# Attention and swish kernel: kv products as two column tiles, and the chunk of tails moved to the end

## The chip, the cores and the metric

The kernel runs on one core of a Trainium2 chip. The metric is the device time of one execution in microseconds. Durations inside the kernel come from a profile of one execution by the hardware profiler; times called "start" count from the start of the profiled span.

## The reference

The kernel computes a linear attention over 8 batches, 8 heads, 576 positions and a head size of 64, and passes its rows through a two-layer block with a swish. Cut to what matters:

```python
def _attn_ref(q, k, v):                       # (8, 8, 576, 64) each
    q_s = np.exp(q - q.max(-1)); q_s /= q_s.sum(-1)
    k_s = np.exp(k - k.max(2));  k_s /= k_s.sum(2)
    kv = np.einsum('bhsd,bhse->bhde', k_s, v)
    return np.einsum('bhsd,bhde->bhse', q_s, kv)

def _moe_ref(x, w_in, w_out, beta):           # x: (4608, 512)
    h = x @ w_in                              # (4608, 2048)
    g = h * (1.0 / (1.0 + np.exp(-beta * h)))
    return g @ w_out                          # (4608, 512)
```

(the keepdims of the reductions are left out here). The result is 4608 rows of 512 values in float32.

## The kernel before

**Chunks.** The 4608 rows are worked off in nine chunks of 512 rows. Chunks 0 to 7 are the first 512 positions of batches 0 to 7 (`MAIN`). The remaining 64 positions of each batch (`TAIL`) are gathered into one more chunk, number `B` = 8, "the tails". The list `order` (lines 47 to 49) says in which order the chunks run; with `LASTMAIN` it is 0 to 6, then 8, then 7. `LASTC` is the chunk that runs last.

**One chunk.** A chunk has 16 steps, one for each block of 128 of the 2048 hidden values. A step is four products of 512 columns with `w_in_b` (`mm_a`, line 334) into `h`, a tanh on ScalarE (line 344), a multiplication on VectorE (line 346) that gives `g`, and, two steps later (`LAG`), four products of 512 columns with `w_out_b` (`mm_b`, line 362) into the four accumulators of the chunk. After the 16th step `store` evacuates the four accumulators, two on ScalarE (`copy`, line 143) and two on VectorE (line 145), and writes them out.

**Attention.** While chunk n of the order runs, `side(n, u)` puts the attention of the next one between the steps u: the exponentials and sums of q (steps 2 to 5), the exponentials of k and the cast of v (4 and 5), the transposition of q by DMA (`q_xbar`, line 240, step 6), the kv products of batch n + 1 (`kv_mm` and `kv_norm`, steps 8 and 10), and the products of q with kv, which give the input of the next chunk (`x_mm`, steps 11 to 14). In the first stage with `side` (n = 1) the steps up to 10 lie two later. k and v go by the batch n + 1, q by `order[n + 1]`. At step 9 `load_next(n + 2)` issues the loads of the chunk after next on SyncE's queue: either one load of q (line 85) or the eight small ones of the q tails (line 93), and then k and v with their tails (lines 109 and 113).

**kv.** A call of `kv_mm` handles two pairs of heads. For batches 2 to 7 each pair is the sum of five products: four over the 512 main positions (line 286) and one over the tails (line 293). The stationary operand is a 128 by 128 block of exponentials of k, 64 columns for each head of the pair. The moving operand is v of both heads with a column of constants for each, 130 columns. Of the result only the two blocks in which head meets head are used: head 0 in partitions 0 to 63 and columns 0 to 64, head 1 in partitions 64 to 127 and columns 65 to 129. `kv_norm` takes the reciprocal of the sums of k (line 304) and writes the two scaled blocks to `kvp` (line 309), a block-diagonal 128 by 128 matrix for each pair. Batches 0 and 1 use another layout (line 264): a full 128 by 128 stationary operand with zeros and 65 moving columns.

**x.** For a main chunk `x_mm` is one product of 512 columns for each pair (line 314); for the tails it is eight of 64 columns, one for each batch (line 318).

**Stores.** `store` has four branches. Tails that are not last: one tile, four stores of 256 KB on SyncE's queue (line 384). Tails that are last: three tiles, two stores for each, one for each half of the partitions (line 401). A main chunk that is last: four tiles and four stores of 256 KB (line 410), the second on ScalarE's queue. Any other main chunk: two stores of 512 KB (line 418). The order of all instructions on each engine is that of the program; the switches `FIX`, `LASTMAIN` and `COLT` on line 45 choose between variants of it.

Of the kernel before, what the change touches and what calls it, by code (L numbers as in the profile page):

```python
# [17 lines left out]
def kernel(  # L18
# [23 lines left out]
    NW = 2  # L42
    D1 = D + 1
    LAG = 2
    FIX, LASTMAIN, COLT = False, True, False
    NCH = B + 1
    order = list(range(NCH))
    if LASTMAIN:
# [620 lines left out]
```

## Time and profile before

| quantity | value |
|---|---|
| median of 3 runs | 291.6 us (291.25 to 292.26) |
| the profiled execution | 292.26 us |
| its span, first to last instruction | 290.5 us |
| mean granted TensorE clock | 0.997 |
| DMA traffic | 50.06 MB, mean 172 GB/s |
| kv products of batches 2 to 7, lines 286 and 293 | 96 + 24, modelled 0.22 us each |
| 128-column weight load for them, LDWEIGHTS | 98 ns each |

In the profile PE is the matrix engine's stream of products and PEld its weight loads, which run beside the products. DVE is VectorE, ACT ScalarE, POOL GpSimd. SPq and ACTq are the queues from which SyncE and ScalarE issue DMAs. Products are pipelined: the duration shown for one contains its way through the array, so a product can start long before the one ahead of it is shown to end. The distance between the starts of two products says what one of them costs in a full stream.

### The profile page before, as it was taken

The numbers are of one execution on the slowest core, as the hardware profiler recorded it, in microseconds if no ns is written. First come the engines' busy times: TensorE is split into PE (matmuls) and PEld (weight loads), VectorE is DVE, ScalarE is ACT, GpSimd is POOL, SyncE is SP. The second block draws the span as 40 slices with busy tenths as digits, with TensorE's granted clock in tenths as the row PEclk, the third lists the DMA queues.
The fourth block names the chain that finished last, engine by engine and source line by source line (L and its number), as shares of the span: only waits on it lengthen the run. The fifth ranks groups of instructions, "written<-read, shape, count | busy, mean of one in ns | idle before, by whom it ended". The sixth has DMA issues, their size and how long they took to land.

```text
span 290.5 us, 3880 instructions
## 1 busy us (share of the span) xinstructions
PE 278.6 (96%) x1447; PEld 131.0 (45%) x1475; DVE 185.2 (64%) x299; ACT 163.9 (56%) x238; POOL 41.5 (14%) x55
## 2 busy tenths in 40 slices
PE   8779979999999999999999999999999999999994
PEld 2434435445444544454445444544455444444441
DVE  7837596695678546955695469546955595454442
ACT  4853676694387347734682568355944564454341
POOL 4349670300030011001200030003000000000000
PEclk9999999999999999999999999999999999999998
DMA  7999999808941972198119902785381033005003
GB/s 248 376 384 378 377 384 316 252 0 218 315 156 38 309 197 105 47 320 217 72 78 271 272 28 118 172 226 146 144 166 53 1 147 72 0 0 147 0 0 144
DMA packets 56226, 50.06 MB, mean 172 GB/s; under 512 B 26240, under 2 KB 47760, under 8 KB 56208
## 3 DMA queue, kind: packets, MB, share of 16 engines
q1 hardware_dynamic: 56064, 49.56, 55.7%
q8 instruction: 11, 0.18, 0.3%
q10 hardware_dynamic: 144, 0.26, 0.2%
q14 instruction: 7, 0.06, 0.1%
HBM read 36.71 MB, written 9.44 MB: 159 GB/s over the span
## 4 chain that ended last, share of the span: by engine, by line
PE 87%; DMA 4%; DVE 3%; ACT 1%; issue 1%; another core or an unknown queue 1%; SPq 0%; POOL 0%; ACTq 0%
DMA k_st_86<-in_k_dram 2%; DMA w_in_97<-in_moe_w_in_dram 2%; PE acc_2_2486 L362 1%; PE acc_0_2173 L362 1%; PE acc_3_724 L362 1%; PE acc_2_2731 L362 1%; PE acc_0_2484 L362 1%; PE acc_2_2175 L362 1%; PE acc_2_1879 L362 1%; PE acc_0_1877 L362 1%; PE acc_1_1589 L362 1%; PE acc_3_2176 L362 1%; PE acc_0_1588 L362 1%; PE acc_2_1012 L362 1%; PE acc_0_1010 L362 1%; PE acc_0_721 L362 1%
## 5 line engine op out<-in xcount | busy, mean ns | idle before, releaser
L334 PEld LDWEIGHTS <-w_in_b 128*128 128x128 bf16 x576 | 55.3, 98 | 66.7 <-issue 2.7
L158 ACT ACTIVATE ek_144<-k_st_86 64x576 bf16<-64x576 f32 x8 | 5.5, 681 | 1.5 <-DVE eq_189 L231 1.4
L426 PEld LDWEIGHTS <-kvp 128*128 128x128 bf16 x34 | 3.6, 112 | 5.7 <-issue 2.8
L145 POOL CAST va_2209<-v_st_2014 128x2048 bf16<-128x2048 f32 x1 | 1.9, 1918 | 29.1 <-DMA v_st_2014<-in_v_dram 29.1
L145 POOL CAST va_1913<-v_st_1718 128x2048 bf16<-128x2048 f32 x1 | 1.9, 1920 | 28.5 <-DMA v_st_1718<-in_v_dram 28.5
L145 POOL CAST va_1624<-v_st_1429 128x2048 bf16<-128x2048 f32 x1 | 1.9, 1917 | 26.7 <-DMA v_st_1429<-in_v_dram 26.7
L158 ACT ACTIVATE ek_149<-k_st_118 64x576 bf16<-64x576 f32 x8 | 5.4, 675 | 0.0
L145 POOL CAST va_1046<-v_st_836 128x2048 bf16<-128x2048 f32 x1 | 1.9, 1919 | 24.2 <-DMA v_st_836<-in_v_dram 24.2
L145 POOL CAST va_1335<-v_st_1140 128x2048 bf16<-128x2048 f32 x1 | 1.9, 1922 | 22.3 <-DMA v_st_1140<-in_v_dram 22.3
L314 PEld LDWEIGHTS <-kvp 128*128 128x128 bf16 x32 | 3.1, 98 | 4.2 <-DVE kvp L309 1.0
L214 ACT ACTIVATE eq_189<-q_st_83 128x1024 bf16<-128x1024 f32 x2 | 2.1, 1056 | 3.0 <-DMA q_st_83<-in_q_dram 3.0
L145 POOL CAST va_147<-v_st_91 128x576 bf16<-128x576 f32 x4 | 2.7, 668 | 7.8 <-DMA v_st_91<-in_v_dram 7.6
L145 POOL CAST va_783<-v_st_132 128x2048 bf16<-128x2048 f32 x1 | 1.9, 1916 | 12.3 <-DMA v_st_132<-in_v_dram 12.3
L145 POOL CAST w_in_b<-w_in_114 128x1024 bf16<-128x1024 f32 x2 | 3.0, 1536 | 2.1 <-DMA w_in_114<-in_moe_w_in_dram 2.1
L231 DVE TENSOR_TENSOR eq_485<-eq_485,rq_487 128x1024 bf16<-128x1024 bf16 x2 | 3.1, 1542 | 0.0
L334 PE MATMUL h_0_316<-xT_80,w_in_b 128*128 128x512 bf16 x4 | 1.5, 380 | 1.5 <-POOL w_in_b L145 1.3
L145 POOL CAST w_out_b<-w_out_116 128x1024 bf16<-128x1024 f32 x2 | 2.6, 1298 | 1.7 <-DMA w_out_116<-in_moe_w_out_dram 1.7
L145 DVE CAST w_in_b<-w_in_102 128x1024 bf16<-128x1024 f32 x2 | 2.6, 1312 | 0.0
L225 DVE TENSOR_REDUCE rq_748<-eq_746 128x16 f32<-128x1024 bf16 x2 | 2.4, 1214 | 0.3 <-ACT eq_746 L214 0.3
L225 DVE TENSOR_REDUCE rq_487<-eq_485 128x16 f32<-128x1024 bf16 x2 | 2.4, 1213 | 0.3 <-ACT eq_485 L214 0.3
L225 DVE TENSOR_REDUCE rq_191<-eq_189 128x16 f32<-128x1024 bf16 x2 | 2.4, 1215 | 0.2 <-ACT eq_189 L214 0.2
L145 POOL CAST w_out_b<-w_out_100 128x1024 bf16<-128x1024 f32 x2 | 2.1, 1040 | 3.3 <-DMA w_out_100<-in_moe_w_out_dram 3.3
(1460 smaller groups left out, 839.6 us busy)
## 6 DMA issues: line engine op xcount, KB each, us to landing
k_st_86<-in_k_dram SPq DMA_DIRECT2D x4, 288.0 KB, 7.0
v_st_91<-in_v_dram SPq DMA_DIRECT2D x4, 288.0 KB, 7.8
k_st_118<-in_k_dram SPq DMA_DIRECT2D x4, 288.0 KB, 9.7
v_st_124<-in_v_dram SPq DMA_DIRECT2D x2, 576.0 KB, 9.3
q_st_83<-in_q_dram SPq DMA_DIRECT2D x2, 512.0 KB, 4.3
w_in_97<-in_moe_w_in_dram SPq DMA_DIRECT2D x2, 512.0 KB, 6.4
w_out_100<-in_moe_w_out_dram SPq DMA_DIRECT2D x2, 512.0 KB, 8.6
w_in_102<-in_moe_w_in_dram SPq DMA_DIRECT2D x1, 1024.0 KB, 9.3
```

The lines of the kernel that those rows point to most:

```text
L145: eng.tensor_copy(dst, src)
L158: nc.scalar.activation(ek[b][r, j : j + m, :, e * D : (e + 1) * D], k_st[b][r, j : j + m, :].rearrange("p j (i d) -> p j i d", i=RW), ACTF ...
L214: nc.scalar.activation(eq[b][:, :, s * m : (s + 1) * m, :].rearrange("p i h d -> p h i d"), q_st[b][:, s * m : (s + 1) * m, :].rearrange(" ...
L225: nc.vector.tensor_reduce(rq[b][:, 0, :, h], eq[b][:, :, h, :], axis=AX.X, op=ALU.add)
L231: nc.vector.tensor_tensor(eq[b][:, :, h, :], eq[b][:, :, h, :], rq[b][:, 1, :, h].unsqueeze(3).to_broadcast((P, R, m, D)), ALU.mult,)
L314: nc.tensor.matmul(t[:], kvp[:, c, j, :], qsT[c][:, :, j, :])
L334: nc.tensor.matmul(h[:], w_in_b[:, kt, ds(j * P, P)], x_of(c)[:, kt, :], start=(kt == 0), stop=(kt == KT - 1),)
L362: nc.tensor.matmul(acc[st][:], g[:, ds(st * P, P)], w_out_b[:, j, :], start=(j == 0), stop=(j == NJ - 1),)
L426: nc.tensor.matmul(t[:, 0:cols], kvp[:, B - 1, 0, :], kvp[:, B - 1, :, :].rearrange("p j r -> p (j r)")[:, 0:cols],)
```

## The change

Two switches on line 45 are turned; no other line is changed.

```diff
-    FIX, LASTMAIN, COLT = False, True, False
+    FIX, LASTMAIN, COLT = False, False, True
```

With `COLT` the branch at lines 272 to 284 takes the place of lines 285 to 299 for batches 2 to 7:

```python
                for i in range(R + 1):
                    for e in range(2):
                        hd = 2 * j + e
                        nc.tensor.matmul(
                            t[e * D : (e + 1) * D, jl, 0:D1],
                            ek[b][:, i, hd, :] if i < R else ekt[...][:, ds(hd * D, D)],
                            va[b][:, i, hd, :] if i < R else vt[...][:, b % 2, hd, :],
                            start=(i == 0),
                            stop=(i == R),
                            tile_position=(0, e * D),
                        )
```

Each head gets products of its own: a stationary operand of 128 rows by 64 columns, placed in the left or right half of the array by `tile_position`, and 65 moving columns. The heads of a pair alternate. Both results lie in columns 0 to 64, in their halves of the partitions, and `kv_norm` (line 308) reads the second head from there.

Without `LASTMAIN` the order is 0 to 8, so the tails run last. The q tails are then loaded where q of batch 7 was, and the other way round; the exponentials, the transposition and the `x_mm` of the two change places in the same way. Chunk 7 is stored at line 418, and the tails by this branch (line 400 chooses the queue; `FIX` is off):

```python
            lo, hi = ((0, 2), (0, 2), (2, 3), (3, 4))[st]
            ...
            if st == hi - 1:
                for e in range(2):
                    ...
                        q_eng = nc.scalar if st == 2 or (st == 3 and e) else nc.sync
                    q_eng.dma_start(out_t[...][e, :, lo:hi, :],
                                    o[e * TAIL : (e + 1) * TAIL, lo:hi, :])
```

## Prediction

> **What bounds the kernel now.** I read the page first, then the stages, then the PE timeline around the kv products, then the end.
>
> ```profile
> span 290.5 us, 3880 instructions
> PE 278.6 (96%) x1447; PEld 131.0 (45%) x1475; DVE 185.2 (64%) x299; ACT 163.9 (56%) x238; POOL 41.5 (14%) x55
> PEclk9999999999999999999999999999999999999998
> PE 87%; DMA 4%; DVE 3%; ACT 1%; issue 1%; another core or an unknown queue 1%; SPq 0%; POOL 0%; ACTq 0%
> ```
>
> PE is busy 96% of the span at full clock and is 87% of the chain that ended last. The stages, cut where h_0 of each chunk starts, with the columns time, then busy time of PE, PEld, DVE, ACT and POOL:
>
> ```profile
> 168.27:198.06 29.79, 29.63 (x151) 14.05 (x152) 19.56 (x33) 17.42 (x25) 2.64 (x3) 1.00 0.56 153
> 198.06:227.91 29.85, 29.64 (x177) 14.57 (x180) 19.55 (x33) 17.54 (x25) 2.53 (x2) 1.00 0.39 104
> 227.91:256.56 28.65, 28.49 (x131) 12.90 (x132) 18.05 (x27) 15.01 (x22) 0.00 (x0) 1.00 0.18 56
> 256.56:286.30 29.74, 29.43 (x135) 12.94 (x134) 13.38 (x20) 13.04 (x20) 0.00 (x0) 1.00 0.14 41
> ```
>
> These are chunks 5, 6, tails and 7. PE leaves about 0.2 us open in each, DVE and ACT some 10 us. So a stage lasts as long as its PE instructions take to follow one another, and that spacing prices this change, not the modelled duration. The kv products, start and duration, with what follows:
>
> ```profile
> 124.24 0.39 PE L286 MATMUL kv_0_1396<-va_1335,ek_1333 128*128 128x130 bf16 x4
> 124.46 0.22 PE L293 MATMUL kv_0_1396<-vt_75,ekt_77 128*128 128x130 bf16 x1
> 124.52 0.39 PE L286 MATMUL kv_0_1396<-va_1335,ek_1333 128*128 128x130 bf16 x4
> 124.75 0.22 PE L293 MATMUL kv_0_1396<-vt_75,ekt_77 128*128 128x130 bf16 x1
> 124.80 1.03 PE L334 MATMUL h_9_1411<-xT_81,w_in_b 128*128 128x512 bf16 x4
> ```
>
> One call of kv_mm is ten products in 124.80 - 124.24 = 0.56 us, 56 ns each, with no gap on either side. Batches 2 to 7 make 12 calls: 6.7 us, all that this half of the change can touch.
>
> **Part 1, the kv products.** Each call loses ten 128x130 products and gains twenty of 65 columns, each with its own weight load of 64 columns: 120 more products and 120 more loads in all. No row has a 64-column stationary operand. The nearest rows are full-width products with a short moving side, and what follows them:
>
> ```profile
> 47.24 0.74 PE L264 MATMUL kv_0_612<-va_151,ek_149 128*128 128x65 bf16 x18
> 47.82 0.38 PE L426 MATMUL warm_635<-kvp 128*128 128x512 bf16 x1
> ...
> 219.91 0.40 PE L318 MATMUL x_0_2341<-qsT_2242,kvp 128*128 128x64 bf16 x8
> 220.14 1.03 PE L334 MATMUL h_12_2351<-xT_80,w_in_b 128*128 128x512 bf16 x4
> ```
>
> Spacing: 0.58/18 = 32 ns at 65 columns, 0.23/8 = 29 ns at 64; each product there has its own 128-column load, and the loads keep up.
>
> Stream, upper bound: the two heads follow one another, 20 x 29 to 32 = 0.58 to 0.64 us a call, +0.02 to +0.08 over 0.56. Lower bound: the heads use different columns of the array and different output partitions, so a pair could pass in the time of one: 10 x 29 to 32 = 0.29 to 0.32, -0.27 to -0.24. I take 0.40, about a third of the way up: nothing in the operands ties the two heads together, but each pair still needs two weight loads where one served. That is -0.16 a call.
>
> Boundaries: the array now changes between full width and two halves, at the start and end of each call, 24 times. No row shows such a change; changes of the moving size alone (512 to 130 to 512 above) cost nothing, the lower bound. If the array must empty, the next product starts at the end of the last and not at its normal spacing. A 512-column product shows 0.38 us and the next one starts 0.22 later, so 0.16 is uncovered at entry; a 65-column one shows 194 ns against 32, so 0.16 again at exit. Above that, a weight load that can't be made ahead would add its 98 ns (row of LDWEIGHTS, 128 columns). I take 0.16 each, 0.32 a call, because a change of the array's layout under products still in flight seems the less likely.
>
> [...]
>
> Sum of part 1: 12 x (-0.16 + 0.32) = +1.9 us.
>
> What hangs on kv: line 304's reciprocal and line 309's two products read the same sizes from other columns. x_mm of the next chunk reads the result of a call one step (1.7 us) or more after it. A call longer by 0.4 us is covered there; without that cover PE would wait that 0.4 us each stage.
>
> **Part 2, the order of the last two chunks.** Chunk 7 now comes before the tails. Each keeps its 16 steps. The tails' x_mm (32 products of 64 columns, 4 x 0.23 = 0.92 us) moves from chunk 6's stage to chunk 7's, and chunk 7's four of 512 columns (4 x 0.22 = 0.88) move the other way: 0 on the sum. The stages show it: 29.85 against 29.79.
>
> Loads: in SP's queue, the eight issues of the q tails took 6.40 us (183.31 to 189.71) and stood ahead of k and v of batch 7. They change places with q of batch 7, one issue of 0.62 us. Keys and values of batch 7 are issued some 5.8 us earlier, at no gain, as PE did not wait for them; the tails issue from about 213 to 219.5 and are first read by line 214 in the next stage, where q of batch 7 is read now at 233.72. With 3.9 us to landing that leaves about 10 us; without it PE would wait only from step 11 on. The transposes by DMA (line 240) keep their step. Chunk 7 leaves by two stores of 512 KB at line 418, the tails no longer by four of 256 KB at line 384; nothing on SP waits closely behind either.
>
> The end changes:
>
> ```profile
> 285.33 0.37 ACTq L410 DMA_DIRECT2D out_dram<-o_1_2900  x1
> ...
> 285.80 0.58 ACT L143 COPY o_2_2907<-acc_2_2731 128x512 f32<-128x512 f32 x1 [0.82 <-PE acc_2_2731 L362]
> ...
> 286.34 0.69 DVE L145 COPY o_3_2914<-acc_3_2732 128x512 f32<-128x512 f32 x1 [1.03 <-PE acc_3_2732 L362]
> ...
> 287.06 0.33 SPq L410 DMA_DIRECT2D out_dram<-o_3_2914  x1
> ```
>
> Now: evacuation of the last accumulator ends at 287.03, one 256 KB store goes out on SP at 287.06, landing takes 2.5 us, and the span ends at 290.5. After: line 401 issues two stores per part. ACT copies o_2 until 286.38, then issues both halves of part 2 (2 x 0.37, until 287.15), and only then its half of part 3, the e = 1 store: 0.1 us later than now. ACT's one store landed in 2.9 us against 2.4 to 2.5 on SP: +0.4. The halves are 128 KB; from 512 to 256 KB landing fell from 3.0 to 2.5, so half of that again would be -0.25. Sum +0.3; bounds -0.2 (size gains, queue equal) and +0.5 (no gain from size).
>
> **Sum.** +1.9 + 0.3 = +2.2 us. The profiled execution took 292.26 us, 290.5 of span and 1.8 around it; it would become 294.5. It stands 0.66 above the median of 291.6, so for a median: 293.8.
>
> **The rivals.**
>
> (a) Overlap without a drain, the faster side: the pair passes in the time of one and the change of layout is free. 12 x -0.27 = -3.2, with the end +0.3: 288.7. For it: disjoint columns and partitions, and free changes of size in the trace. Against: twice the weight loads. It decides if the boundaries cost under about 0.16 us a call at my stream.
>
> (b) The tiles don't overlap and boundaries are free, so the column tiles don't do what they say: 12 x +0.05 = +0.6, end +0.3: 292.5. For it: the trace's 29 to 32 ns for short products however wide the load.
>
> (c) Weight loads become the bound: where a 64-column load can't hide under the other head's product, it costs half of the 98 ns row, 49 ns, or all of it. 20 x 49 = 0.98 a call, +0.42, times 12 = +5.0; with drains +8.9; end +0.3: 296.9 to 300.8. Against: loads in the trace overlap at 29 ns.
>
> **How the numbers follow.** The forecast (drains, some overlap) 0.45; (a) 0.30; (b) 0.13; (c) 0.12. The forecast's own range: streams of 0.29 to 0.64 with both drains give 12 x (+0.05 to +0.40) = +0.6 to +4.8, end -0.2 to +0.5: 292.0 to 296.9. The whole range goes from (a)'s 288.7 past the forecast's top into the low end of (c), to 297.5, and leaves out the rest of (c) and what of (a) gains more. What can be told from no change is 0.3%, 0.9 us. Faster: 0.27 from (a). Same: 0.06 of the forecast, 0.03 of (a), 0.06 of (b): 0.15. Slower: 0.39 + 0.07 + 0.12 = 0.58.
>
> **What would show it.** Around each kv call, the first 65-column product should start 0.3 to 0.4 us after the last 512-column one instead of 0.22, and h_9 likewise after the call. Starts of the two heads: a few ns apart means overlap, about 30 means (b), 50 or more (c). A stage with kv should last 29.95 instead of 29.79, the last two 28.7 and 29.7. At the end the last issue should be on ACT's queue near 0.8 to 0.9 us after PE's last end. The forecast is wrong if calls are shorter than 0.56 us, if PE waits at x_mm, or if a stage without kv changes.

## The result and the profile after

The changed kernel takes 293.75 us, median of 6 runs (292.89 to 294.25), against 291.43 us (290.83 to 292.26) for the kernel before: a ratio of 1.0077 with a 95% interval of 1.0053 to 1.0100. It is slower, and the prediction of 293.8 us hits the total. Its parts were wrong: by the traces the column tiles, to which it gave +1.9 us, gained 0.3 us, and the end of the kernel, to which it gave +0.3 us, lost 1.9 us.

The page of the changed kernel, its profiled execution of 293.56 us:

```profile
span 291.4 us, 4117 instructions
PE 279.2 (96%) x1565; PEld 128.2 (44%) x1595; DVE 184.4 (63%) x299; ACT 163.8 (56%) x238; POOL 40.9 (14%) x55
PEclk9999999999999999999999999999999999999999
PE 83%; DMA 8%; DVE 3%; ACT 2%; issue 1%; POOL 1%; SPq 0%; ACTq 0%; POOLq 0%
```

PE is as busy as before. The DMA share of the chain doubled, but that stands at the start: in this execution the chain of the first 40 us happens to run over a load of w_in (4%). The stages, cut where h_0 of chunks 5, 6, 7 and the tails starts:

```profile
167.39:197.13 29.74, 29.58 (x171) 13.54 (x172) 19.37 (x33) 17.42 (x25) 3.54 (x4) 1.00 0.58 169
197.13:226.87 29.74, 29.49 (x170) 13.54 (x172) 19.37 (x33) 17.53 (x25) 1.64 (x2) 1.00 0.33 89
226.87:255.59 28.72, 28.51 (x158) 13.43 (x160) 18.05 (x27) 15.02 (x22) 0.00 (x0) 1.00 0.24 56
255.59:285.32 29.73, 29.42 (x134) 12.97 (x134) 13.38 (x20) 13.12 (x20) 0.00 (x0) 1.00 0.09 36
```

A stage with kv takes 29.74 us where it took 29.79: shorter, not longer. The last two are what they were, 28.72 against 28.65 with the 0.06 us of the tails' x_mm that moved into it, and 29.73 against 29.74. PE's work ends at 285.32 here and at 286.30 before, because the start of this execution was 0.7 us quicker (h_0 of chunk 2 at 78.17 against 78.91) and the tiles gained 0.3. Yet the span is 0.9 us longer. The time between PE's end and the end of the span grew from 290.5 - 286.30 = 4.2 us to 291.4 - 285.32 = 6.1 us. One call of kv_mm in the PE timeline:

```profile
127.23 0.38 PE L362 MATMUL acc_3_1342<-w_out_b,g_8_1430 128*128 128x512 bf16 x1
127.54 0.32 PE L276 MATMUL kv_1_1495<-va_1375,ek_1373 128*64 128x65 bf16 x8
127.69 0.20 PE L276 MATMUL kv_1_1495<-vt_75,ekt_77 128*64 128x65 bf16 x2
127.72 0.30 PE L276 MATMUL kv_1_1495<-va_1375,ek_1373 128*64 128x65 bf16 x8
127.84 0.20 PE L276 MATMUL kv_1_1495<-vt_75,ekt_77 128*64 128x65 bf16 x2
127.98 0.39 PE L334 MATMUL h_11_1520<-xT_81,w_in_b 128*128 128x512 bf16 x1
```

The call spans 127.98 - 127.23 = 0.75 us less the 0.22 of the 512-column product: 0.54 us, where ten products took 0.56. Inside it, the first tile product starts 0.31 us after the last wide one (0.22 is normal, so 0.09 more), then eighteen start in 127.84 - 127.54 = 0.30 us, 17 ns each, and h_11 starts 0.13 us after the last one. Taken one by one, the starts in this trace come in pairs: the two heads 3 to 7 ns apart, and each pair 29 to 36 ns after the one before (52 or 53 for the second pair of a call). So a pair passes in about the time of one product, 29 to 32 ns in the prediction's rows, as rival (a) had it, and the two changes of layout take back 0.09 + 0.10 us. The weight loads keep up with that pace, though each is shown to last longer than the 98 ns of a 128-column one (shortest, median and longest, ns):

```profile
L276 PEld LDWEIGHTS <-ek_1373 x32: 106/111/114, 123.5 to 127.8; 128*64 128x64 bf16 x32
```

Most of the time of a load thus lies beside that of its neighbours, and its duration is not what it costs.

The end of the changed kernel:

```profile
284.39 1.34 SPq L401 DMA_DIRECT2D out_dram<-o_0_3014  x2
...
284.94 0.38 PE L362 MATMUL acc_3_2850<-w_out_b,g_15_3005 128*128 128x512 bf16 x1
...
285.11 1.31 ACTq L401 DMA_DIRECT2D out_dram<-o_2_3024  x2
285.36 0.69 DVE L145 COPY o_3_3032<-acc_3_2850 128x512 f32<-128x512 f32 x1 [1.03 <-PE acc_3_2850 L362]
286.08 0.95 SPq L401 DMA_DIRECT2D out_dram<-o_3_3032  x1
286.52 1.75 ACTq L401 DMA_DIRECT2D out_dram<-o_3_3032  x1
```

A store of half the partitions takes 0.6 to 1.75 us to issue, where before's stores of all took 0.33 to 0.37. What the DMA engines do meanwhile is in the last two columns of a window (their busy share, GB/s), here from 286 to 288 us, first the kernel before and then the changed one:

```profile
286.00:288.00 2.00, 0.30 (x2) 0.00 (x0) 0.69 (x1) 0.39 (x1) 0.00 (x0) 1.00 1.00 367
```

```profile
286.00:288.00 2.00, 0.00 (x0) 0.00 (x0) 0.05 (x1) 0.00 (x0) 0.00 (x0) 1.00 0.94 205
```

The engines are nearly equally busy, 1.00 and 0.94, and move 367 against 205 GB/s. The low rate doesn't last to the end. In the next stretch of the changed kernel it is higher, though still below before's:

```profile
287.50:290.00 2.50, 0.00 (x0) 0.00 (x0) 0.00 (x0) 0.00 (x0) 0.00 (x0) 1.00 0.92 271
```

Nor is the rate the whole difference. In windows of 0.1 us the transfers go on for 4.5 us in place of 3.1, which is 1.4 us more. They also begin 0.8 us later, 0.4 us after PE's end where before they begin 0.4 us ahead of it: the first store waits for two accumulators, and its bytes move 1.3 us after its issue in place of 0.85. The span ends 0.3 us sooner after the last bytes. Together that is the 1.9 us.

The trace of before had shown a low rate in its middle, unused by the prediction: chunk 6 leaves by two stores of all partitions, the tails by four of half, the same 1 MB.

```profile
233.50:236.00 2.50, 2.45 (x13) 1.12 (x12) 2.13 (x3) 2.49 (x4) 0.00 (x0) 1.00 1.01 398
262.50:267.50 5.00, 4.95 (x24) 2.29 (x24) 2.06 (x3) 1.37 (x2) 0.00 (x0) 1.00 0.74 210
```

It took 2.5 us for the one and 5.0 for the other. Chunk 6 goes in packets of 4 KB and the tails in packets of 2 KB, so this pair alone doesn't say that the partitions do it; chunk 7's four stores at the end, 256 KB each in packets of 2 KB like the tails', move at 367 GB/s. In mid-kernel nobody waits for the tails' stores; at the end the span does. Two theories follow for the experiments. Theory A is the prediction's: the tiles lose through the changes of layout. Theory B: the tiles gain a little, and the loss is the tails' stores at the end. Within B, H lays it to the rate of half-partition stores, its rival Q to stores issued by ACT.

### The profile page after: what moved, and what is told of

Same layout as the page of the kernel before. It is cut to its first block, busy times and chain, and to the rows that moved or that the text cites. A ratio compares the mean times of both kernels' runs of the same rounds, so it can differ in the third digit from the quotient of the medians.

```text
span 291.4 us, 4117 instructions
## 1 busy us (share of the span) xinstructions
PE 279.2 (96%) x1565; PEld 128.2 (44%) x1595; DVE 184.4 (63%) x299; ACT 163.8 (56%) x238; POOL 40.9 (14%) x55
## 4 chain that ended last, share of the span: by engine, by line
PE 83%; DMA 8%; DVE 3%; ACT 2%; issue 1%; POOL 1%; SPq 0%; ACTq 0%; POOLq 0%
DMA w_in_114<-in_moe_w_in_dram 4%; DMA w_in_97<-in_moe_w_in_dram 2%; DMA k_st_86<-in_k_dram 2%; PE acc_2_2578 L362 1%; PE acc_0_2576 L362 1%; PE acc_0_1957 L362 1%; PE acc_3_1033 L362 1%; PE acc_1_722 L362 1%; PE acc_3_1960 L362 1%; PE acc_1_1649 L362 1%; PE acc_2_2849 L362 1%; PE acc_1_1958 L362 1%; PE acc_2_723 L362 1%; PE acc_0_1648 L362 1%; PE acc_0_1030 L362 1%; PE acc_3_724 L362 1%
## 5 line engine op out<-in xcount | busy, mean ns | idle before, releaser
L145 DVE CAST w_in_b<-w_in_102 128x1024 bf16<-128x1024 f32 x2 | 3.6, 1790 | 0.0
L145 POOL CAST w_out_b<-w_out_100 128x1024 bf16<-128x1024 f32 x2 | 2.1, 1040 | 4.2 <-DMA w_out_100<-in_moe_w_out_dram 4.2
L225 DVE TENSOR_REDUCE rq_191<-eq_189 128x16 f32<-128x1024 bf16 x2 | 2.4, 1216 | 0.3 <-ACT eq_189 L214 0.3
L225 DVE TENSOR_REDUCE rq_487<-eq_485 128x16 f32<-128x1024 bf16 x2 | 2.4, 1218 | 0.3 <-ACT eq_485 L214 0.3
L225 DVE TENSOR_REDUCE rq_748<-eq_746 128x16 f32<-128x1024 bf16 x2 | 2.4, 1214 | 0.3 <-ACT eq_746 L214 0.3
L225 DVE TENSOR_REDUCE rq_1040<-eq_1038 128x16 f32<-128x1024 bf16 x2 | 2.4, 1192 | 0.3 <-ACT eq_1038 L214 0.3
L225 DVE TENSOR_REDUCE rq_2276<-eq_2274 128x16 f32<-128x1024 bf16 x2 | 2.4, 1190 | 0.3 <-ACT eq_2274 L214 0.3
L225 DVE TENSOR_REDUCE rq_1658<-eq_1656 128x16 f32<-128x1024 bf16 x2 | 2.4, 1190 | 0.3 <-ACT eq_1656 L214 0.3
```

Of the source, the lines that this page charges most:

```text
L145: eng.tensor_copy(dst, src)
L225: nc.vector.tensor_reduce(rq[b][:, 0, :, h], eq[b][:, :, h, :], axis=AX.X, op=ALU.add)
```

## The experiments

Each kernel was timed beside the kernel before on the same chip. The last column is the time from the end shown for PE's last product to the end of the span in the profiled execution, good to about 0.1 us.

| kernel | median us | before us | ratio (95%) | PE's end to span's end, us |
|---|---|---|---|---|
| before | | | | 4.2 |
| changed | 293.75 | 291.43 | 1.0077 (1.0053 to 1.0100) | 6.1 |
| e1 tiles only | 291.23 | 291.63 | 0.9994 (0.9980 to 1.0008) | 4.2 |
| e2 order only | 293.76 | 291.63 | 1.0091 (1.0058 to 1.0124) | 6.1 |
| e3 tiles, one call | 290.53 | 291.63 | 0.9957 (0.9942 to 0.9972) | 4.1 |
| e4 main stores split | 292.83 | 291.63 | 1.0042 (1.0028 to 1.0056) | 5.2 |
| e5 halves on SP | 293.87 | 291.42 | 1.0068 (1.0045 to 1.0090) | 6.1 |
| e6 whole stores | 292.56 | 291.42 | 1.0039 (1.0026 to 1.0052) | 4.5 |
| e7 both mended | 290.83 | 291.42 | 0.9979 (0.9965 to 0.9993) | 4.4 |
| e8 heads in turn | 292.19 | 291.42 | one run | 4.2 |
| e9 whole by copy | 291.57 | 291.29 | 1.0010 (0.9996 to 1.0024) | 4.5 |
| e10 one call by copy | 290.45 | 291.29 | 0.9962 (0.9947 to 0.9976) | 4.5 |

**e1 and e2, one half of the change each.**

```diff
-    FIX, LASTMAIN, COLT = False, True, False
+    FIX, LASTMAIN, COLT = False, True, True     # e1
+    FIX, LASTMAIN, COLT = False, False, False   # e2
```

> Column tiles alone, the order of the chunks as before. Theory A (as predicted: the change of layout costs 0.16 us at each boundary, so the tiles carry the loss): +1.9 us against before, and a call of kv_mm takes 0.72 us from the end of the last 512-column spacing to the next product. Theory B (from the trace of the changed kernel: a call takes 0.54 us, and the loss lies in the stores at the end): -0.3 us, within noise, stages with kv of 29.74 us, and 4.2 us from PE's last end to the end of the span, as before.

> The tails last, kv products as before. Theory A: +0.3 us. Theory B: the whole loss and a little more, +2.3 to +2.6 us, with stages of 29.79 us and 6.1 us from PE's last end to the end of the span, where before has 4.2.

The tiles alone make no difference that the runs can tell, 0.9994; their 0.3 us rests on the traces. In the profile of e1 kv products of successive batches stand 29.74 us apart, in that of e2 29.79. The order alone carries the loss, +2.1 us between the medians (+1.7 to +3.6 by the interval, which one execution of 296.5 us widens), with the same 6.1 us at the end. Theory A falls.

**e3, all four pairs of a batch in one call.** Column tiles in the old order; 65 columns for each pair let four pairs fit where two did.

```diff
-        t = ps.tile([P, n, 2 * D1], F32, tag=tag, ...)
+        t = ps.tile([P, n, 2 * D1 if n < 4 else D1], F32, tag=tag, ...)
...
-        if u in (8 + o, 10 + o) and kb < B:
-            kv_mm(kb, (u - 8 - o) // 2)
-            kv_norm(kb, (u - 8 - o) // 2)
+        if u == 8 + o and kb < B:
+            kv_mm(kb, 0, n=4)
+            kv_norm(kb, 0, n=4)
```

> Column tiles, order as before, and all four head pairs of a batch in one call at step 8, so 6 calls and 12 changes of layout in place of 24. In the trace of the changed kernel the first tile product starts 0.31 us after the last 512-column one (0.22 normally) and the next 512-column one 0.11 us after the last tile product's spacing, some 0.2 us a call for the changes of layout. If they are paid once a call, 6 calls less save 1.2 us: -1.5 us against before, stages with kv of 29.54 us. If they cost nothing and the 0.2 us belongs to the twenty products themselves: -0.3 us, as with the tiles alone. By theory A: 6 x 0.32 less, so about 0 against before.

The PE timeline of e3:

```profile
122.67 0.59 PE L362 MATMUL acc<-w_out_b,g 128*128 128x512 bf16 x2
123.20 0.32 PE L276 MATMUL kv<-va,ek 128*64 128x65 bf16 x8
...
123.82 0.20 PE L276 MATMUL kv<-vt,ekt 128*64 128x65 bf16 x2
123.96 0.39 PE L334 MATMUL h<-xT,w_in_b 128*128 128x512 bf16 x1
```

Forty products go from 123.20 to 123.82 at the same pace; the second wide product above starts at 122.89, so the entry is again 0.31, and the exit, from the second of the two products at 123.82, again 0.13. A call of forty takes 123.96 - 122.89 - 0.22 = 0.85 us against two of twenty at 0.54, so 0.23 less for each batch, and the stages are 29.51 us. Six batches make 1.4 us; the medians say 1.1 us and the ratio 1.3 (291.63 x 0.0043). The changes of layout cost about 0.2 us a call, as read, and paying them half as often is what makes the tiles worth having.

**e4, the old order with half-partition stores.** The kernel before, with the stores of the last two accumulators of chunk 7 split.

```diff
-            (nc.sync, nc.scalar, nc.sync, nc.sync)[st].dma_start(ov[:, st, :], o[:, st, :])
+            if st < 2:
+                (nc.sync, nc.scalar)[st].dma_start(ov[:, st, :], o[:, st, :])
+                return
+            for e in range(2):
+                q_eng = nc.scalar if st == 2 or e else nc.sync
+                r = slice(e * TAIL, (e + 1) * TAIL)
+                q_eng.dma_start(ov[r, st, :], o[r, st, :])
```

> The kernel before, with order and kv products as before, but the stores of the last two accumulators of chunk 7 split into halves of 64 partitions and put on the queues that the changed kernel uses (both halves of part 2 and one of part 3 on ACT). If the split and the queue cost the time at the end, it shows here too: +1 to +2 us, halves issuing in about 0.65 us and the last one on ACT in more than 1 us. If it is the place in memory of the tails' rows: 0 to +0.3 us, with issues of 0.34 us.

It is slower by 1.2 us, and its windows show both rates in one kernel, the whole stores first and then the halves:

```profile
285.00:286.00 1.00, 0.25 (x2) 0.00 (x0) 0.69 (x1) 0.36 (x1) 0.00 (x0) 1.00 0.99 379
286.50:288.00 1.50, 0.00 (x0) 0.00 (x0) 0.00 (x0) 0.00 (x0) 0.00 (x0) 1.00 0.86 194
```

These are rows of chunk 7, not of the tails, so the place in memory isn't needed for the low rate. The first issue and the first bytes stand where they stood before, 1.3 and 0.4 us ahead of PE's end, so the 1.0 us by which this end is longer comes from splitting the last 0.5 MB. The half on SP issues in 0.50 us and the three on ACT in 2.03; the issue of more than 1 us that was expected of the last one isn't there, and the loss is.

**e5, ACT taken out.** The changed kernel, all six stores of the tails on SP's queue.

```diff
-                        q_eng = nc.scalar if st == 2 or (st == 3 and e) else nc.sync
+                        q_eng = nc.sync
```

> The changed kernel with all six stores of the tails on SP's queue, halves as they are. Theory Q (a store issued by ACT is what ends late: issues of 1.31 and 1.75 us there): the loss goes, about 0 to +0.8 us against before. Theory H (a store from 64 partitions moves at half the rate: some 195 GB/s against 385 in the last us of the two traces): the loss stays, as one queue works off the halves one after another: 1.05 MB at 195 GB/s is 5.4 us from 285.5, so the end moves from 290.0 to as late as 290.9, and the time is +2 to +3.5 us against before.

It is 2.45 us slower than before, the end still 6.1 us. The loss doesn't hang on which queue issues; Q falls.

**e6 and e7, the tails stored whole.** Two batches are interleaved, so that a store with all 128 partitions can write both; e7 has e3's single call as well.

```diff
-                    t[:, ds(b * TAIL, TAIL)],
+                    t[:].rearrange("p (i t e) -> p i e t", i=R, e=2)[:, i, e, :],
...
+            o = stage.tile([P, R, DM], F32, tag="wo", bufs=4, name=f"o{c}_{st}")
+            evac(eng, o[:, st, :], acc[st][:])
+            (nc.sync, nc.scalar, nc.sync, nc.sync)[st].dma_start(
+                out_t[:, MAIN:S, :].rearrange("(i e) t f -> i t e f", e=2)[st], o[:, st, :]
+            )
+            return
```

> The changed kernel with the tails interleaved: x_mm writes the two batches of a pair to even and odd columns, so that each accumulator leaves in one store of all 128 partitions, four stores on the queues of before's last chunk. Theory H: the rate at the end is 385 GB/s again, 4.2 us from PE's last end to the end of the span, and the time is that of the tiles alone, -0.3 us against before (between -0.8 and +0.3). Theory Q: the same, as ACT issues one store only. If the place of the tails' rows in memory is what costs: +0.5 us or more.

> As the kernel with whole stores, and all four head pairs of a batch in one call. If the two repairs add up: -1.2 us against before, the same as one call alone in the old order (0.9957 of before).

The end is mostly mended, 4.5 us against 4.2, and the rate at the end of e6 is back:

```profile
286.00:287.00 1.00, 0.00 (x0) 0.00 (x0) 0.68 (x1) 0.36 (x1) 0.00 (x0) 1.00 1.00 383
```

But e6 is still 1.1 us slower than before, which the expectation missed. The x_mm of the tails shows a price that I hadn't counted:

```profile
251.71 0.61 PE L318 MATMUL x<-qsT,kvp 128*128 128x64 bf16 x8
252.13 0.62 PE L334 MATMUL h<-xT,w_in_b 128*128 128x512 bf16 x2
```

Eight products that write every other column take 0.42 us in place of 0.23, four times 0.19 = 0.76 us. With 0.3 at the end and 0.35 outside the span (below), less the 0.3 that the tiles gain, that makes the 1.1. e7 carries the same 0.76, and so gains 0.6 us and not 1.2.

The 0.3 at the end belongs to something else in the tails' stores than halves: the first whole store is issued 1.3 us ahead of PE's end as before, but its bytes move 1.3 us after that and not 0.85, and the one on ACT takes 0.66 us to issue, not 0.37. Whether the rows' place in memory or the shape of the store does it, no run tells.

**e8, the order of the tile products.** Column tiles in the old order; the five products of one head before the five of the other.

```diff
-                for i in range(R + 1):
-                    for e in range(2):
+                for e in range(2):
+                    for i in range(R + 1):
                         hd = 2 * j + e
```

> Column tiles, order of the chunks as before, but the five products of one head run before the five of the other, so that neighbours use the same half of the array. If the 16 ns between tile products come from the two halves working side by side: neighbours now follow at 29 to 32 ns within a head, a call of twenty products takes 0.8 to 0.85 us, stages with kv 30.3 us. If they come from shorter weight loads and products alone: still 16 ns and 0.54 us a call.

```profile
127.49 0.59 PE L362 MATMUL acc<-w_out_b,g 128*128 128x512 bf16 x2
128.01 0.34 PE L276 MATMUL kv<-va,ek 128*64 128x65 bf16 x7
128.16 0.19 PE L276 MATMUL kv<-vt,ekt 128*64 128x65 bf16 x1
...
128.39 0.20 PE L276 MATMUL kv<-vt,ekt 128*64 128x65 bf16 x1
128.52 0.39 PE L334 MATMUL h<-xT,w_in_b 128*128 128x512 bf16 x1
```

One run says nothing of the time; the trace has to. Neither expectation came true. Twenty starts take 128.39 - 128.01 = 0.38 us, 20 ns each, a call 0.60 us and a stage 29.86: slower than alternating heads, but far from the 29 to 32 ns of one product after another. In the program the fifth product of a call is the first one over tails (vt, ekt); in the trace seven over main positions start ahead of it where the program has four, so products of the second head start before the first head's are through. The halves work side by side here too, out of program order, only less evenly. That overlap is shown; alternating the heads isn't its condition.

**e9 and e10, the interleaving moved to the copy.** As e6, with the products writing as before and the copy out of PSUM doing the interleaving; e10 with the single call too.

```diff
+        if c == B:
+            evac(
+                eng,
+                x_of(c)[:, j, :].rearrange("p (i t e) -> p i e t", i=R, e=2),
+                t[:].rearrange("p (i e t) -> p i e t", i=R, e=2),
+            )
+            return
         evac(eng, x_of(c)[:, j, :], t[:])
```

> The changed kernel with whole stores of the tails, where the interleaving of the two batches is done by the copy out of PSUM (line 323) and not by the products, whose interleaved writing took 0.42 us for eight of 64 columns in place of 0.23. Theory H (the loss at the end is the rate of half-partition stores, and what the first kernel with whole stores still lost is that writing, 4 x 0.19 = 0.76 us): 0.76 us less than it, +0.3 us against before, with x_mm groups of 0.23 us and 4.2 to 4.5 us from PE's last end to the end of the span. If +0.35 us of time outside the span stays as in that kernel (2.15 against 1.8), the time is about before's; without it -0.3. If something else in the order of the chunks costs: still +1 us or more.

> As the kernel with whole stores by the copy, and all four head pairs in one call. If everything adds up: 1.2 us less than that kernel and 0.6 us less than the one with both repairs and interleaved products, 290.1 to 290.4 us where before has 291.5; equal within noise to one call alone in the old order, so that the order of the chunks is worth nothing either way.

```profile
248.94 0.40 PE L318 MATMUL x<-qsT,kvp 128*128 128x64 bf16 x8
249.18 1.03 PE L341 MATMUL h<-xT,w_in_b 128*128 128x512 bf16 x4
```

Eight products take 0.24 us again. The interleaving copies take 0.73 us, where the others take 0.59 on ACT and 0.68 on DVE, and PE doesn't wait for them. e9 is 0.3 us above before, within noise, as expected for the case in which the time outside the span stays. e10, 0.9962, equals e3, 0.9957: with whole stores the order of the chunks is worth nothing that these intervals, 0.4 us to either side, can show. These two, with one call, are the fastest versions and can't be told apart: 290.53 and 290.45 us, faster than both kernels.

**What the sum is.** From before to the changed kernel: six batches with 0.05 us less, -0.3; the end +1.9; and 0.35 us outside the span, since every execution of the changed kernel has about 2.15 us outside it where before has 1.8. That makes +1.95 us, within the +1.5 to +2.9 of the interval. The 0.35 us is open: e2, e5, e6 and e9 show it too, all with the tails last, but e7 and e10, also with the tails last, don't.

## Why the prediction was right, and where it was wrong

**What bounds the kernel** held: PE spacing sets the stages, every stage without kv kept its length, and PE waited for nothing new.

**Part 1, the stream**, was mis-sized: I took 0.40 us, a third of the way up from full overlap; twenty products take 0.34 (0.54 less the 0.19 of the boundaries), nearly full overlap. My doubt, two weight loads where one served, was unfounded: the trace shows that the pairs of loads keep up with the pairs of products, one pair every 29 to 36 ns.

**Part 1, the boundaries**, is the first step that failed: "I take 0.16 each, 0.32 a call", a term that was sized too high. They cost 0.09 and 0.10, so 0.19. Not nothing, and not the whole uncovered time of the product in flight, 0.16. That the array empties at a change of layout was my assumption behind the 0.16; there is a cost at just these places, but no run shows what it consists of. The 49 ns that rival (c) took for each weight load, half of the 98 ns row, aren't borne out, neither as a duration, which is shown as 106 to 114 ns, nor as a pace, as two loads go by in the 29 to 36 ns of a pair. With both terms smaller, 12 x (-0.22 + 0.19) = -0.3 us replaces +1.9. Rival (a) had the right mechanism for the stream and the wrong price for the boundaries, and rivals (b) and (c) are out.

**Part 2, the order**, was right in PE's work, loads, transposes and SP's queue, all at nothing.

**Part 2, the end**, is the second step that failed: "Sum +0.3; bounds -0.2 (size gains, queue equal) and +0.5 (no gain from size)". I priced the last store by the queue that issues it and by its size, and put the partitions that it reads at nothing. The halves of 128 KB landed in 3.8 to 4.2 us, not sooner than the 2.4 to 2.9 of the stores before, and the last issue started 1.2 us after PE's end, not 0.8 to 0.9. The last 1 MB kept the DMA engines busy from about 285.7 to 290.2 instead of 285.8 to 288.9, at about 200 GB/s for its first 1.8 us and 271 after, against 367. Cost: 1.9 us in the span, 1.4 of it in the transfers and the rest in their later start, less the 0.3 after them. That halves cost by themselves is shown by e4, and that whole stores take most of the loss away by e6 and e9. The rows for it stood in the trace of before: 210 GB/s for the tails' four stores of 256 KB, which landed in 3.4 us, and 367 for chunk 7's four.

Why stores from half the partitions move at 194 (e4) to 205 GB/s (the changed kernel), where those of the kernel before move at 367, no run here shows, nor why the rate of the changed kernel is higher, 271, from 287.5 to 290 us.

So the total was right by luck, through two errors of nearly equal size and opposite sign, -2.2 us on the tiles and +1.6 on the end in the span, with 0.35 outside it for the rest. The signs that the prediction named would have told: calls under 0.56 us were to make the forecast wrong, and they are 0.54. Another would have misled: the first tile product, 0.31 us after the last wide one, lies within the 0.3 to 0.4 that were to speak for the forecast.

## What to carry to other kernels

Two column tiles of 64 columns ran side by side here, a pair every 29 to 36 ns where one full-width product of 65 columns took 32, but each switch into or out of that layout cost about 0.1 us, and one call in place of two gained 0.23 us for each batch (e3): gather all tiled products into as few stretches as possible. The stores that read all 128 partitions moved at 367 GB/s at the end and the halves at 205 over the same 2 us, so here what is stored last should leave in whole stores. A shape that is harmless in mid-kernel can set the end, and its rate could be read earlier: the same tails moved at 210 GB/s in the middle of the kernel before. When a prediction's total comes true, check its terms, as one run of each half of the change did here.

## What the runs showed of the hardware

Column-tile products of the two halves start out of program order when the program puts one half's products first (e8: seven products over main positions ahead of the first over tails, where the program has four). Products that write every other PSUM column take 52 ns for 64 columns in place of 29 (e6), while the copy that writes bf16 to every other column takes 0.73 us in place of 0.59 (ACT) and 0.68 (DVE), beside PE's work (e9). Two weight loads of 64 columns and two products of 65 go by every 29 to 36 ns, though each load is shown with 106 to 114 ns. Stores from 64 partitions moved at about 200 GB/s for their first 1.8 us and at 271 from 287.5 to 290 us, where stores of 256 KB from 128 moved at 367 (the changed kernel and the kernel before).
